# Wide lengths of q, and expert maxima row by row, in a fused attention and expert-routing kernel

## The chip, the cores and the metric

The program runs on one core of a Trainium2 chip. The metric is device time in microseconds (us) of one execution. TensorE is PE in the profile (PEld its weight loads), VectorE DVE, ScalarE ACT, GpSimd POOL and SyncE SP.

## What is computed

```
qn = q / (norm(q, axis=1) + 1e-6);  kn likewise          # q, k, v: 4 x 5056 x 256
s  = kn^T @ qn / tau                                     # 256 x 256 for each batch
a  = softmax(s, -1);  x = v @ a                          # 20224 tokens of 256
logits = x @ w_gate                                      # 8 experts
# pairs (token, expert) by falling logit: a token goes to the first expert that
# has room (2528 places each)
out[tokens of e] = relu(x @ w1[e]) @ w2[e]
```

## The kernel before

**Scores.** Four batches b run one after another. A batch has ten tiles of k and q (4 x 128 tokens each, buffers `ua` and `uc`). For each tile PE multiplies k by q into `s` (L334), ACT squares k and q (L344, L347) and DVE adds the squares into `acc_k` and `acc_q` (L348); L352 and L353 fold these to one row of 256. The lengths of batch b follow when the first tile of batch b+1 is in (`late(norms_before)`, L339).

**Lengths** (`norms`, L355, and `lengths`, L365). Four matmuls against a column of ones (L358) leave the 256 sums of k and the 256 of q as four columns, one sum a partition. On these 128x4 values run a copy out of PSUM (L361), a square root on ACT (L367), a step of Newton's rule on POOL and DVE (L368 to L373, the first reciprocal is L370), a second reciprocal (L375) and the factor 1/tau (L376).

**Softmax** (`softmax`, L379). The lengths of q are needed along the free axis. DVE makes two diagonals of them (L385), PE multiplies these by ones (L386) and ACT copies the result (L387). Then DVE scales the scores (L391), takes the row maximum, and works out the exponential as a polynomial (L396 to L405), the sums (L408) and the quotient `ac` (L414). PE turns `ac` (L422, `turned_a`), multiplies by the gate weights (L431, `gates`), ACT rounds it to `aH`, and DVE forms the rest `aL` (L249), which PE needs for x = v @ a (L283, with v split into `vh` and `vl`, L262). The transpose of batch 0 is put behind the last tile of batch 1, that of batch 3 stands behind all scores and the logits of one set of columns (L446).

**Order of the attention part.** The tile framework orders each engine's queue by its own estimates. All queues are served in order, and the softmax of batch b stands in DVE's queue among the additions of batch b+1.

**Routing** (`route`, L568). For R = 8, 7, ... 2 experts left: `m` is the maximum over R rows of logits L (L582); `eq` marks which row has it (L602), is multiplied by the codes 8, 7, ... of the rows (L604) and reduced to `f`, the code of a token's best expert (L607); `oh` is its one-hot form (L626 or L616). A search by 15 thresholds a round, with totals counted by 20 small matmuls (L699), finds which expert fills first and where. That expert's row is taken out by copying L to a second tile L2 (L876, L878). `compact` then lists its tokens.

**Order of the expert part.** From the last 26 tiles of x on, an `Order` object (L1035) plans by hand: each step of the routing names its engine and an estimated cost (`ve`, `vi`), and the plan puts it between the matmuls of the experts (`layer1` L1333, `layer2` L1365). x goes to DRAM (`store_x`) and is gathered by expert (L1225); the first expert can start when the last store has landed. 27 matmuls (L1313) stand in between.

Of the kernel before, what the change touches and what calls it, by code (L numbers as in the profile page):

```python
# [21 lines left out]
E, F = 8, 1024  # L22
# [69 lines left out]
def attention_moe(ctx: ExitStack, tc: tile.TileContext, q, k, vt, tau, wg, w1t, w2t, tabs, out):  # L92
# [74 lines left out]
    dmask = const.tile([128, CG, E], F32, name="dmask")  # L167
    V.tensor_scalar(dmask, jrow[:, 0:CG, None].to_broadcast([128, CG, E]), pc_, None, op0=OP.is_equal)
# [16 lines left out]
    scale = const.tile([128, 4], F32, name="scale")  # L185

    L2 = state.tile([128, E, COLS], F32, name="L1")
    U01 = state.tile([128, COLS], F32, name="U01")
    state.tile([128, 16], F32, name="pad_s")
# [108 lines left out]
    with ExitStack() as sctx:  # L298
# [12 lines left out]
        def scores(b, extra, norms_before):  # L311
# [183 lines left out]
        def load_scale():  # L495
            V.reciprocal(scale[:, 0:2], tau_t.to_broadcast([128, 2]))
            V.memset(scale[:, 2:4], 1.0)
# [70 lines left out]
    def route(p, R):  # L568
        nonlocal L, L2, U01, asg, ne, ne2
# [9 lines left out]
        else:  # L579
            m = rtile("m")  # L580
            yield ve(R * COLS)
            V.tensor_reduce(m, L[:, 0:R].rearrange("p r c -> p c r"), axis=AX.X, op=OP.max)  # L582
# [273 lines left out]
        if R > 1:  # L856
# [398 lines left out]
    def turn(p, c):  # L1255
# [4 lines left out]
        if not xts:  # L1260
            ffx.tile([128, 48], F32, name="pad_x", bufs=1)
# [299 lines left out]
```

## Time and profile before

| | us |
|---|---|
| median of 3 runs (lowest, highest) | 1256.83 (1256.02, 1259.64) |
| the profiled execution | 1257.59 |
| its span in the trace | 1255.8 |
| scores, softmax, x and logits up to the first routing step on DVE | 0 to 223 |
| the rest of x, the first expert's routing, the gather | 223 to 321 |
| experts | 321 to 1256 |

A row of the timeline gives start, length (of a pipelined instruction up to its end, so that rows overlap), engine, line, operation, output<-inputs, shapes, count, and in brackets the idle time before it and what ended that. A row of the groups gives busy time and mean nanoseconds of one.

### The profile page before, as it was taken

The numbers are of one execution on the slowest core, as the hardware profiler recorded it, in microseconds if no ns is written. First come the engines' busy times: TensorE is split into PE (matmuls) and PEld (weight loads), VectorE is DVE, ScalarE is ACT, GpSimd is POOL, SyncE is SP. The second block draws the span as 40 slices with busy tenths as digits, with TensorE's granted clock in tenths as the row PEclk, the third lists the DMA queues.
The fourth block names the chain that finished last, engine by engine and source line by source line (L and its number), as shares of the span: only waits on it lengthen the run. The fifth ranks groups of instructions, "written<-read, shape, count | busy, mean of one in ns | idle before, by whom it ended". The sixth has DMA issues, their size and how long they took to land.

```text
span 1255.8 us, 24082 instructions
## 1 busy us (share of the span) xinstructions
PE 1238.3 (99%) x8779; PEld 1111.2 (88%) x8779; DVE 872.7 (69%) x2457; ACT 601.0 (48%) x1441; POOL 384.5 (31%) x690
## 2 busy tenths in 40 slices
PE   8999999999999999999999999999999999999998
PEld 6888977898888988998999899988989898898998
DVE  6688496898778778868867888887785445344431
ACT  6646652467324434434533755556554554334331
POOL 1000010000432353244343452532444434334322
PEclk9999999999999999999999999999999999999999
DMA  8999875236112134143422532341434235333301
GB/s 308 314 409 414 311 275 199 118 153 235 58 48 87 41 84 121 42 90 81 126 68 59 138 79 64 80 131 40 93 73 129 59 80 146 73 69 76 69 31 34
DMA packets 184759, 160.33 MB, mean 128 GB/s; under 512 B 150080, under 2 KB 155328, under 8 KB 180032
## 3 DMA queue, kind: packets, MB, share of 16 engines
q1 hardware_dynamic: 157712, 79.33, 22.6%
q0 software_dynamic: 17664, 58.22, 14.4%
q10 hardware_dynamic: 9264, 21.24, 4.4%
q8 instruction: 69, 1.13, 0.4%
q14 instruction: 50, 0.41, 0.1%
HBM read 99.97 MB, written 41.68 MB: 113 GB/s over the span
## 4 chain that ended last, share of the span: by engine, by line
PE 84%; DVE 6%; issue 5%; POOL 2%; DMA 2%; ACT 1%; SPq 0%; POOLq 0%; DVEq 0%; ACTq 0%
PE ph L1333 33%; PE py L1365 32%; PE px L283 7%; PE s L334 7%; PE pc L699 2%; POOL out_dram L1372 1%; PE px L446 1%; DVE acc_q L348 1%; PE pi L912 1%; DVE yy L405 1%; DVE acc_k L348 1%; DMA x_d<-xs 1%; DMA ua<-in_q_dram 1%; DVE vl L262 0%; ACT ua L1184 0%
## 5 line engine op out<-in xcount | busy, mean ns | idle before, releaser
L1333 PE MATMUL ph<-xH,ua 128*128 128x512 f32 (+3 forms) x1312 | 354.8, 388 | 0.3 <-ACT xH L1300 0.3
L1365 PE MATMUL py<-uc,hH 128*128 128x256 f32 (+1 forms) x2560 | 334.5, 279 | 0.0
L1341 DVE SCALAR_TENSOR_TENSOR hL<-ph,hH 128x512 fp32r<-128x512 f32 (+3 forms) x328 | 219.4, 670 | 162.4 <-ACT hH L1336 158.2
L1365 PEld LDWEIGHTS py<-uc,hH 128*128 128x128 f32 (+1 forms) x2560 | 312.9, 187 | 2.2
L1372 POOL DMA_INDIRECT out_dram<-y,idx x160 | 162.0, 1013 | 498.1 <-ACT y L1370 445.3
L1336 ACT ACTIVATE hH<-ph 128x512 fp32r<-128x512 f32 (+3 forms) x328 | 190.6, 582 | 206.1 <-PE ph L1333 202.1
L1333 PEld LDWEIGHTS ph<-xH,ua 128*128 128x128 f32 x1312 | 238.4, 189 | 42.8 <-ACT xH L1300 0.4
L1333 PE MATMUL ph<-xL,ua 128*128 128x512 f32 (+3 forms) x656 | 201.3, 386 | 0.1
L1370 ACT ACTIVATE y<-py 128x256 f32<-128x256 f32 (+1 forms) x160 | 61.3, 383 | 251.0 <-PE py L1365 235.1
L1225 POOL DMA_INDIRECT xg<-x_d,src x156 | 156.6, 1004 | 71.6 <-issue 33.6
L1365 PE MATMUL py<-uc,hL 128*128 128x256 f32 (+1 forms) x1280 | 178.3, 280 | 0.0
L1365 PEld LDWEIGHTS py<-uc,hL 128*128 128x128 f32 (+1 forms) x1280 | 160.2, 187 | 0.0
L1333 PEld LDWEIGHTS ph<-xL,ua 128*128 128x128 f32 x656 | 122.1, 189 | 23.3 <-DVE xL L1303 0.3
L334 PE MATMUL s<-ua 128*128 128x256 f32 x320 | 73.7, 387 | 2.6 <-DMA ua<-in_q_dram 2.6
L334 PEld LDWEIGHTS s<-ua 128*128 128x128 f32 x320 | 61.0, 193 | 14.2 <-issue 3.4
L286 ACT ACTIVATE xs<-px 128x512 f32<-128x512 f32 (+1 forms) x96 | 49.4, 528 | 49.5 <-PE px L283 47.8
L334 PE MATMUL s<-uc 128*128 128x256 f32 x320 | 71.3, 380 | 0.0
L334 PEld LDWEIGHTS s<-uc 128*128 128x128 f32 x320 | 60.3, 190 | 8.8 <-issue 0.8
L283 PE MATMUL px<-aH,vh 128*128 128x256 f32 (+1 forms) x216 | 62.7, 292 | 0.0
L283 PE MATMUL px<-aH,vl 128*128 128x256 f32 (+1 forms) x216 | 61.3, 284 | 1.1 <-DVE vl L262 0.9
L1284 DVE TENSOR_TENSOR xL<-ph,xH 128x512 fp32r<-128x512 f32 (+1 forms) x66 | 42.9, 679 | 27.8 <-ACT xH L1281 25.7
L969 ACT ACTIVATE junk<-pi,rhalf 128x160 bf16<-128x160 f32 x140 | 54.0, 391 | 15.7 <-PE pi L912 14.6
(341 smaller groups left out, 1569.5 us busy)
## 6 DMA issues: line engine op xcount, KB each, us to landing
x_d<-xs ACTq DMA_DIRECT2D x39, 512.0 KB
xq<-xg SPq DMA_DIRECT2D x500, 32.0 KB
vr<-in_vt_dram SPq DMA_DIRECT2D x14, 1024.0 KB
uc<-in_k_dram SPq DMA_DIRECT2D x18, 512.0 KB
uc<-in_q_dram SPq DMA_DIRECT2D x18, 512.0 KB
ua<-in_k_dram SPq DMA_DIRECT2D x17, 512.0 KB
ua<-in_q_dram SPq DMA_DIRECT2D x17, 512.0 KB
out_dram<-y,idx POOLq DMA_INDIRECT x160, 2.4
```

The costliest lines, as they stand in the source:

```text
L283: mm = PE.matmul(px[:, i * C:i * C + width], lhsT=l_, rhs=a_, start=(j == 0), stop=(j == len(terms) - 1))
L286: S.activation(xs[:, t % TH:t % TH + n, 0:width], px[:, 0:n * width].rearrange("p (t c) -> p t c", t=n), AF.Copy)
L334: newest[0] = PE.matmul(sb[:, ib * C:(ib + 1) * C], lhsT=kt[:, t, ib * 128:(ib + 1) * 128], rhs=qt[:, t, :], start=(first and t == 0 and i ...
L969: S.activation(junk, pi[:, i * W:i * W + COLS], AF.Sign, bias=rhalf[:, g0 + i:g0 + i + 1], scale=-1.0, accum_out=sgn[:, g0 + i:g0 + i + 1])
L1225: P.indirect_dma_start(out=xg[:n, i, :], out_offset=None, in_=x_d, in_offset=bass.IndirectOffsetOnAxis(ap=at, axis=0))
L1284: V.tensor_tensor(xL[:, kb, 0:nt], pt[:, 0:nt], xH[:, kb, 0:nt].bitcast(F32), op=OP.subtract)
L1333: PE.matmul(ph[:, 0:nt], lhsT=l[:, w], rhs=x_[:, kb, 0:nt], start=(i == 0), stop=(i == 5))
L1336: S.activation(hH[:, fb, 0:nt], ph[:, 0:nt], AF.Relu)
L1341: V.scalar_tensor_tensor(hL[:, fb, 0:nt], ph[:, 0:nt], 0.0, hH[:, fb, 0:nt].bitcast(F32), op0=OP.max, op1=OP.subtract)
L1365: PE.matmul(py[:n, 0:C], lhsT=l[:, fb, tk], rhs=w[:, d], start=(j == 0), stop=(j == 23))
L1370: S.activation(y[:n], py[:n, 0:C], AF.Copy)
L1372: sd = P.indirect_dma_start(out=out, out_offset=bass.IndirectOffsetOnAxis(ap=idx[:n, col:col + 1], axis=0), in_=y[:n], in_offset=None)
```

## The change

Five edits. (1) `norms`: the sums of k stay two matmuls; the sums of q are made by one matmul with a 128x128 block of ones as weights, so that all partitions hold all 256 sums. (2) `lengths` runs on 128x258 values, with POOL keeping one of its five steps and DVE taking the rest; the diagonals, their matmuls and ACT's copy leave `softmax`. (3) `route`: the maxima over experts are trees of pairwise maxima (`tallest`), the codes and the one-hot rows are made by one instruction a row, `f` is bf16 and `oh` lies by rows in all rounds (which changes the operands of L699). (4) The finished row is taken out of L in place, without copy and without L2. (5) Small tiles for alignment change size.

```diff
             def norms():
                 pn = pcnt.tile([128, 512], F32, name="pc")
-                for i, (acc, ib) in enumerate(((acc_k, 0), (acc_k, 1), (acc_q, 0), (acc_q, 1))):
-                    newest[0] = PE.matmul(pn[:, i:i + 1], lhsT=acc[:, 0, ib * 128:(ib + 1) * 128], rhs=ones_f[:, 0:1],
-                                          start=True, stop=True)
-                nrm = wk.tile([128, 4], F32, name="nrm", bufs=2)
-                V.tensor_copy(nrm, pn[:, 0:4])
-                cur["rn"] = lengths(nrm)
+                for ib in range(2):
+                    PE.matmul(pn[:, ib:ib + 1], lhsT=acc_k[:, 0, ib * 128:(ib + 1) * 128], rhs=ones_f[:, 0:1],
+                              start=True, stop=True)
+                newest[0] = PE.matmul(pn[:, 2:2 + C], lhsT=ones_f, rhs=acc_q[:, 0], start=True, stop=True)
+                cur["rn"] = lengths(pn[:, 0:2 + C])
...
-        def lengths(nrm):
-            y = wk.tile([128, 4], F32, name="ny", bufs=2)
-            S.activation(y, nrm, AF.Sqrt)
+        def lengths(sums):
+            W = 2 + C
+            nrm = wk.tile([128, 2, C], F32, name="z").rearrange("p a c -> p (a c)")[:, 0:W]
+            V.tensor_copy(nrm, sums)
+            y = wk.tile([128, 2, C], F32, name="yy").rearrange("p a c -> p (a c)")[:, 0:W]
+            S.activation(y, sums, AF.Sqrt)
             P.tensor_scalar(y, y, 1.0e-30, None, op0=OP.max)
-            d = wk.tile([128, 4], F32, name="nd", bufs=2)
+            d = wk.tile([128, W], F32, name="rn")
             V.reciprocal(d, y)
-            P.tensor_tensor(d, d, nrm, op=OP.mult)
-            P.tensor_tensor(y, y, d, op=OP.add)
-            P.tensor_scalar(y, y, 0.5, 1.0e-6, op0=OP.mult, op1=OP.add)
-            rn = wk.tile([128, 4], F32, name="rn", bufs=2)
-            V.reciprocal(rn, y)
-            P.tensor_tensor(rn, rn, scale, op=OP.mult)
-            return rn
+            V.tensor_tensor(d, d, nrm, op=OP.mult)
+            V.tensor_tensor(y, y, d, op=OP.add)
+            V.tensor_scalar(y, y, 0.5, 1.0e-6, op0=OP.mult, op1=OP.add)
+            V.reciprocal(d, y)
+            V.tensor_tensor(d[:, 0:2], d[:, 0:2], scale, op=OP.mult)
+            return d
 
         def softmax(sb, rn):
             nf = wk.tile([128, 2, C], F32, name="nf")
-            dq = nf[:, 0].rearrange("p (j i) -> p j i", j=2)
-            rq = nf[:, 1]
-            pq = pcnt.tile([128, 512], F32, name="pc")
-            for jb in range(2):
-                V.tensor_scalar(dq[:, jb], ident, rn[:, 2 + jb:3 + jb], None, op0=OP.mult)
-                PE.matmul(pq[:, jb * 128:(jb + 1) * 128], lhsT=ones_f, rhs=dq[:, jb], start=True, stop=True)
-            S.activation(rq, pq[:, 0:C], AF.Copy)
+            rq = rn[:, 2:2 + C]
...
+    def tallest(out, rows, part, n, rate):
+        while n > 2:
+            h = (n + 1) // 2
+            yield ve(h * COLS, rate)
+            V.tensor_tensor(part[:, 0:h], rows[:, 0:h], rows[:, n - h:n], op=OP.max)
+            rows, n = part, h
+        yield ve(COLS)
+        V.tensor_tensor(out, rows[:, 0], rows[:, n - 1], op=OP.max)
...
-            V.tensor_reduce(m, L[:, 0:R].rearrange("p r c -> p c r"), axis=AX.X, op=OP.max)
+            top = rtile("eq", (128, E * COLS), BF).bitcast(F32).rearrange("p (r c) -> p r c", c=COLS)
+            yield from tallest(m, L, top, R, 1)
...
-            V.tensor_tensor(eq[:, 0:R], eq[:, 0:R], code9[:, 0:R, None].to_broadcast([128, R, COLS]), op=OP.mult)
-            f = rtile("f")
-            yield ve(R * COLS)
-            V.tensor_reduce(f, eq[:, 0:R].rearrange("p r c -> p c r"), axis=AX.X, op=OP.max)
+            for q in range(min(R, E - 1)):
+                yield (vi if q else ve)(COLS, 4)
+                V.tensor_scalar(eq[:, q], eq[:, q], float(E - q), None, op0=OP.mult)
+            f = rtile("f", dt=BF)
+            yield from tallest(f, eq, eq, R, 2)
...
+            oh = rtile("eq", (128, E * COLS), BF).rearrange("p (r c) -> p r c", r=E)
+            for q in range(Q):
+                yield (vi if q else ve)(COLS, 4)
+                V.tensor_scalar(oh[:, q], f, float(E - q), None, op0=OP.is_equal)
...
-                    PE.matmul(D, lhsT=ge[:, g], rhs=oh[:, cs_, 0:Q], start=(g == 0), stop=(g == COLS // CG - 1))
+                    PE.matmul(D, lhsT=ge[:, g], rhs=oh[:, 0:Q, cs_], start=(g == 0), stop=(g == COLS // CG - 1))
...
-            V.tensor_copy(L2[:, 0:R - 1], L[:, 1:R])
             yield ve((R - 1) * COLS)
-            V.copy_predicated(L2[:, 0:R - 1], keep[:, 0:R - 1, None].to_broadcast([128, R - 1, COLS]),
-                              L[:, 0:R - 1])
+            V.copy_predicated(L[:, 0:R - 1], drop[:, 0:R - 1, None].to_broadcast([128, R - 1, COLS]), L[:, 1:R])
```

DVE's queue behind the sums of batch 0, where its lengths are worked out among the additions of batch 1. Before:

```order
L361 COPY nrm<-pc 128x4
L348 TENSOR_TENSOR acc_k<-acc_k,sq 128x1024
L370 RECIPROCAL nd<-ny 128x4
L348 TENSOR_TENSOR acc_q<-acc_q,sq 128x1024
L375 RECIPROCAL rn<-ny 128x4
```

With the change (all lines from there on stand six lower):

```order
L366 COPY z<-pc 128x258
L347 TENSOR_TENSOR acc_k<-acc_k,sq 128x1024
L371 RECIPROCAL rn<-yy 128x258
L347 TENSOR_TENSOR acc_q<-acc_q,sq 128x1024
L372 TENSOR_TENSOR rn<-rn,z 128x258
L347 TENSOR_TENSOR acc_k<-acc_k,sq 128x1024
L373 TENSOR_TENSOR yy<-yy,rn 128x258
L347 TENSOR_TENSOR acc_q<-acc_q,sq 128x1024
L374 TENSOR_SCALAR yy<-yy 128x258
L347 TENSOR_TENSOR acc_k<-acc_k,sq 128x1024
L375 RECIPROCAL rn<-yy 128x258
```

The chain of the lengths has seven instructions on DVE in place of five, all but one 258 wide, with an addition behind nearly each of them.

The end of the same softmax on DVE, up to the folding of batch 1's sums (`acc_k`, `acc_q`). Before:

```order
L408 SCALAR_TENSOR_TENSOR yy,sm<-yy,pw 128x256 x2
L410 TENSOR_SCALAR sm<-sm 128x2
L348 TENSOR_TENSOR acc_k<-acc_k,sq 128x1024
L411 RECIPROCAL sm<-sm 128x2
L414 TENSOR_SCALAR ac<-yy,sm 128x256 x2
L348 TENSOR_TENSOR acc_q<-acc_q,sq 128x1024
L348 TENSOR_TENSOR acc_k<-acc_k,sq 128x1024
L348 TENSOR_TENSOR acc_q<-acc_q,sq 128x1024
L352 TENSOR_TENSOR acc_k<-acc_k 128x512
```

With the change:

```order
L402 SCALAR_TENSOR_TENSOR yy,sm<-yy,pw 128x256 x2
L347 TENSOR_TENSOR acc_q<-acc_q,sq 128x1024
L404 TENSOR_SCALAR sm<-sm 128x2
L351 TENSOR_TENSOR acc_k<-acc_k 128x512
L405 RECIPROCAL sm<-sm 128x2
L351 TENSOR_TENSOR acc_q<-acc_q 128x512
L408 TENSOR_SCALAR ac<-yy,sm 128x256 x2
L352 TENSOR_TENSOR acc_k<-acc_k 128x256
```

`ac` of batch 0 now stands behind every addition of batch 1; three of them stood behind it.

PE's queue where batch 0 ends and batch 1 begins, up to the transpose of `ac` (L422, now L416). Before:

```order
L358 MATMUL pc<-ones_f,acc_k 128x1 x2
L358 MATMUL pc<-ones_f,acc_q 128x1 x2
L334 MATMUL s<-uc 128x256 x8
L334 MATMUL s<-ua 128x256 x4
L386 MATMUL pc<-nf,ones_f 128x128 x2
L334 MATMUL s<-ua 128x256 x12
L334 MATMUL s<-uc 128x256 x16
L334 MATMUL s<-ua 128x256 x16
L334 MATMUL s<-uc 128x256 x16
L422 MATMUL pm<-ident,ac 128x128 x4
L334 MATMUL s<-ua 128x256 x8
```

With the change:

```order
L357 MATMUL pc<-ones_f,acc_k 128x1 x2
L359 MATMUL pc<-acc_q,ones_f 128x256
L333 MATMUL s<-uc 128x256 x8
L333 MATMUL s<-ua 128x256 x16
L333 MATMUL s<-uc 128x256 x16
L333 MATMUL s<-ua 128x256 x16
L333 MATMUL s<-uc 128x256 x16
L416 MATMUL pm<-ident,ac 128x128 x4
L333 MATMUL s<-ua 128x256 x8
```

The two matmuls of the diagonals are gone; the transpose keeps its place behind the last tile of batch 1.

## Rows read from the trace of the kernel before

**Rows 1.** The page, its first part: engines, busy time, share of the span.
```profile
PE 1238.3 (99%) x8779; PEld 1111.2 (88%) x8779; DVE 872.7 (69%) x2457; ACT 601.0 (48%) x1441; POOL 384.5 (31%) x690
```

**Rows 2.** PE's waits: who waited for whom, total, times, longest.
```profile
PE pc L386 <- DVE nf L385: 1.9, 2, 1.3
...
PE px L283 <- DVE vl L262: 0.9, 1, 0.9
```

**Rows 3.** Busy time of the engines by stretches of 20 us.
```profile
60.00:80.00 20.00, 20.00 (x95) 17.60 (x94) 19.93 (x36) 9.43 (x10) 0.61 (x1) 1.00 1.02 401
...
160.00:180.00 20.00, 20.00 (x117) 13.59 (x110) 19.97 (x31) 12.39 (x13) 1.68 (x2) 1.00 0.87 306
```

**Rows 4.** DVE's timeline, lengths of batch 0 to `aL` of batch 0.
```profile
47.66 0.16 DVE L361 COPY nrm<-pc 128x4 f32<-128x4 f32 x1 [7.49 <-PE pc L358]
...
79.39 0.62 DVE L414 TENSOR_SCALAR ac<-yy,sm 128x256 f32<-128x256 f32 x2
...
84.94 0.42 DVE L353 TENSOR_TENSOR acc_q<-acc_q 128x256 f32<-128x256 f32 x1
...
91.47 0.71 DVE L249 TENSOR_TENSOR aL<-ac,aH 128x528 fp32r<-128x528 f32 x1
```

**Rows 5.** PE's timeline of the same stretch.
```profile
54.18 0.68 PE L386 MATMUL pc<-nf,ones_f 128*128 128x128 f32 x4 [1.27 <-DVE nf L385]
...
80.60 0.60 PE L422 MATMUL pm<-ident,ac 128*128 128x128 f32 x4
...
85.17 0.58 PE L358 MATMUL pc<-ones_f,acc_k 128*128 128x1 f32 x4 [0.42 <-DVE acc_k L353]
...
92.29 0.33 PE L283 MATMUL px<-aL,vh 128*128 128x264 f32 x1
```

**Rows 6.** All instructions of lines L370 and L411: ns shortest/median/longest.
```profile
L370 DVE RECIPROCAL nd<-ny x4: 178/178/179, 50.2 to 195.5; 128x4 f32<-128x4 f32 x4
...
L411 DVE RECIPROCAL sm<-sm x4: 150/157/166, 79.2 to 211.8; 128x2 f32<-128x2 f32 x4
```

**Rows 7.** Groups of DVE's instructions by line and form: busy us, mean ns.
```profile
L348 DVE TENSOR_TENSOR acc_k<-acc_k,sq 128x1024 f32<-128x1024 f32 x36 | 43.8, 1216 | 19.3 <-ACT sq L347 18.3 <-ACT acc_k L344 1.0
...
L582 DVE TENSOR_REDUCE m<-L 128x160 f32<-128x1280 f32 x1 | 2.4, 2397 | 0.1
...
L385 DVE TENSOR_SCALAR nf<-ident,rn 128x128 f32<-128x128 f32 x8 | 2.0, 282 | 0.7 <-POOL rn L376 0.6
...
L410 DVE TENSOR_SCALAR sm<-sm 128x2 f32<-128x2 f32 x4 | 0.6, 162 | 0.1
```

**Rows 8.** Timeline of DVE and PE, lengths of batch 2 to `ac` of batch 3.
```profile
156.01 0.16 DVE L361 COPY nrm<-pc 128x4 f32<-128x4 f32 x1 [8.58 <-PE pc L358]
...
192.09 0.42 DVE L353 TENSOR_TENSOR acc_q<-acc_q 128x256 f32<-128x256 f32 x1
...
193.70 0.50 PE L358 MATMUL pc<-ones_f,acc_k 128*128 128x1 f32 x4
...
199.66 0.87 DVE L391 SCALAR_TENSOR_TENSOR z<-s,rn,nf 128x256 f32<-128x256 f32 x2 [2.12 <-ACT nf L387]
...
212.48 0.81 PE L422 MATMUL pm<-ident,ac 128*128 128x128 f32 x4 [0.28 <-DVE ac L414]
```

**Rows 9.** Single us around the first expert: PE busy first, granted clock third from last.
```profile
320.00:321.00 1.00, 0.55 (x4) 0.41 (x4) 1.00 (x1) 0.54 (x2) 0.00 (x0) 1.00 0.00 0
...
323.00:324.00 1.00, 1.00 (x7) 1.00 (x6) 0.51 (x2) 0.46 (x2) 0.65 (x1) 0.50 0.00 0
326.00:327.00 1.00, 1.00 (x9) 1.00 (x8) 0.77 (x2) 0.42 (x2) 0.57 (x2) 0.83 0.00 0
```

**Rows 10.** Timeline: ACT's last copy of x, POOL's first gather.
```profile
311.56 0.60 ACT L286 ACTIVATE xs<-px 128x512 f32<-128x512 f32 x1 [0.61 <-PE px L283]
...
316.08 0.95 POOL L1225 DMA_INDIRECT xg<-x_d,src  x1 [23.50 <-DVE eq L602]
```

**Rows 11.** The page's chain of work that ended last: its time by line.
```profile
PE ph L1333 33%; PE py L1365 32%; PE px L283 7%; PE s L334 7%; PE pc L699 2%; POOL out_dram L1372 1%; PE px L446 1%; DVE acc_q L348 1%; PE pi L912 1%; DVE yy L405 1%; DVE acc_k L348 1%; DMA x_d<-xs 1%; DMA ua<-in_q_dram 1%; DVE vl L262 0%; ACT ua L1184 0%
```

More of the change, by code (lines that the diff above doesn't have):

```diff
@@ L166, in attention_moe @@
     V.memset(jsel[:, NT:J], 0.0)
-    dmask = const.tile([128, CG, E], F32, name="dmask")
-    V.tensor_scalar(dmask, jrow[:, 0:CG, None].to_broadcast([128, CG, E]), pc_, None, op0=OP.is_equal)
+    dmask = const.tile([128, CG], F32, name="dmask")
+    V.tensor_scalar(dmask, jrow[:, 0:CG], pc_, None, op0=OP.is_equal)
     th0 = const.tile([128, NT, CG], I16, name="th0")
@@ L184, in attention_moe @@
     tau_t = const.tile([128, 1], F32, name="tau_t")
-    scale = const.tile([128, 4], F32, name="scale")
-    L2 = state.tile([128, E, COLS], F32, name="L1")
+    scale = const.tile([128, 2], F32, name="scale")
     U01 = state.tile([128, COLS], F32, name="U01")
-    state.tile([128, 16], F32, name="pad_s")
+    state.tile([128, 72], F32, name="pad_s")
     asg = state.tile([128, COLS], F32, name="asg")
@@ L495, in load_scale @@
         def load_scale():
-            V.reciprocal(scale[:, 0:2], tau_t.to_broadcast([128, 2]))
-            V.memset(scale[:, 2:4], 1.0)
+            V.reciprocal(scale, tau_t.to_broadcast([128, 2]))
         cur = {}
@@ L568, in route @@
     def route(p, R):
-        nonlocal L, L2, U01, asg, ne, ne2
+        nonlocal L, U01, asg, ne, ne2
         r = {}
@@ L602, in route @@
             V.tensor_tensor(eq[:, 0:R], L[:, 0:R], m[:, None, :].to_broadcast([128, R, COLS]), op=OP.is_equal)
-            yield ve(R * COLS)
-            V.tensor_tensor(eq[:, 0:R], eq[:, 0:R], code9[:, 0:R, None].to_broadcast([128, R, COLS]), op=OP.mult)
-            f = rtile("f")
-            yield ve(R * COLS)
-            V.tensor_reduce(f, eq[:, 0:R].rearrange("p r c -> p c r"), axis=AX.X, op=OP.max)
+            for q in range(min(R, E - 1)):
[3 more added lines that the diff above has]
+            yield from tallest(f, eq, eq, R, 2)
             yield ve(COLS)
@@ L611, in route @@
             Q = R if few else R + R % 2
-            flat = rtile("eq", (128, E * COLS), BF)
-            yield ve(Q * COLS)
+            oh = rtile("eq", (128, E * COLS), BF).rearrange("p (r c) -> p r c", r=E)
+            for q in range(Q):
+                yield (vi if q else ve)(COLS, 4)
+                V.tensor_scalar(oh[:, q], f, float(E - q), None, op0=OP.is_equal)
             if few:
-                oh = flat.rearrange("p (r c) -> p r c", r=E)
-                V.tensor_tensor(oh[:, 0:R], f[:, None, :].to_broadcast([128, R, COLS]),
-                                code9[:, 0:R, None].to_broadcast([128, R, COLS]), op=OP.is_equal)
                 need = rtile("need", (128, E))
@@ L624, in route @@
             else:
-                oh = flat.rearrange("p (c r) -> p c r", r=E)
-                V.tensor_tensor(oh[:, :, 0:Q], f[:, :, None].to_broadcast([128, COLS, Q]),
-                                code9[:, None, 0:Q].to_broadcast([128, COLS, Q]), op=OP.is_equal)
                 Ex = rtile("Ex", (128, J, E), F32R)
@@ L694, in totals @@
                 pc = pcnt.tile([128, 512], F32, name="pc")
-                D = pc[:, 0:CG * Q]
+                D = pc[:, 0:Q * CG].rearrange("p (r c) -> p r c", c=CG)
                 yield "P", COLS * Q / 2.4 + 3 * COLS / CG + 60
@@ L698, in totals @@
                     cs_ = slice(g * CG, (g + 1) * CG)
-                    PE.matmul(D, lhsT=ge[:, g], rhs=oh[:, cs_, 0:Q], start=(g == 0), stop=(g == COLS // CG - 1))
+                    PE.matmul(D, lhsT=ge[:, g], rhs=oh[:, 0:Q, cs_], start=(g == 0), stop=(g == COLS // CG - 1))
                 yield ve(CG * Q, psum=True)
-                Dm = rtile("Dm", (128, CG, E))
-                V.tensor_tensor(Dm[:, :, 0:Q], D.rearrange("p (c r) -> p c r", r=Q), dmask[:, :, 0:Q], op=OP.mult)
+                Dm = rtile("Dm", (128, E, CG))
+                V.tensor_tensor(Dm[:, 0:Q], D, dmask[:, None, :].to_broadcast([128, Q, CG]), op=OP.mult)
                 yield ve(CG * Q)
                 Dr = rtile("Dr", (128, E))
-                V.tensor_reduce(Dr[:, 0:Q], Dm[:, :, 0:Q].rearrange("p c r -> p r c"), axis=AX.X, op=OP.add)
+                V.tensor_reduce(Dr[:, 0:Q], Dm[:, 0:Q], axis=AX.X, op=OP.add)
                 yield ve(J * Q)
@@ L797, in route @@
             V.tensor_scalar(one, code9, cs, None, op0=OP.is_equal)
-            keep = rtile("keep", (128, 8), I32)
+            drop = rtile("drop", (128, 8), I32)
             yield ve(8)
-            V.tensor_scalar(keep, code9[:, 0:8], cs, None, op0=OP.is_gt)
+            V.tensor_scalar(drop, code9[:, 0:8], cs, None, op0=OP.is_le)
             Gf = rtile("Gf")
@@ L871, in route @@
             yield ve(16)
-            V.tensor_copy(ne2[:, :, 0:8], o9[:, :, 1:9])
+            V.tensor_copy(ne2[:, :, 0:8], o9[:, :, 0:8])
             yield ve(16)
-            V.copy_predicated(ne2[:, :, 0:8], keep[:, None, :].to_broadcast([128, 2, 8]), o9[:, :, 0:8])
-            yield ve((R - 1) * COLS, 2)
-            V.tensor_copy(L2[:, 0:R - 1], L[:, 1:R])
+            V.copy_predicated(ne2[:, :, 0:8], drop[:, None, :].to_broadcast([128, 2, 8]), o9[:, :, 1:9])
             yield ve((R - 1) * COLS)
-            V.copy_predicated(L2[:, 0:R - 1], keep[:, 0:R - 1, None].to_broadcast([128, R - 1, COLS]),
-                              L[:, 0:R - 1])
-            L, L2, ne, ne2 = L2, L, ne2, ne
+            V.copy_predicated(L[:, 0:R - 1], drop[:, 0:R - 1, None].to_broadcast([128, R - 1, COLS]), L[:, 1:R])
+            ne, ne2 = ne2, ne
     def compact(p):
@@ L1259, in turn @@
         nt = n_of(p, c)
-        if not xts:
-            ffx.tile([128, 48], F32, name="pad_x", bufs=1)
         xH = ffx.tile([128, 2, 512], F32R, name="xH")
```

## The prediction

> **What bounds the kernel now.** I read the page's busy times first: PE is busy 99% of the span, DVE 69% [rows 1]. So the time can fall only by what PE idles or runs at half clock, or by fewer columns on PE. The list of PE's waits says how little there is to win where the change works: 1.9 us in all at the diagonals (L386), 0.9 us for `vl` [rows 2]. The busy times by stretches say the opposite about risk: between 60 and 80 us DVE is busy 19.93 us of 20, between 160 and 180 us 19.97 [rows 3]. There DVE is as full as PE, and has kept up only just. The average of 69% hides it, since it comes from the experts' part. What the change adds on DVE in these stretches is not covered; it moves what PE waits for.
>
> Which waits end last there? The timelines of DVE and PE, batch 0's lengths to its `aL`, show it [rows 4, 5]. DVE makes `ac` at 79.39 us, and PE comes to its transpose at 80.60: about 0.6 us to spare. `aL` starts at 91.47 and takes 0.71; PE's first matmul with it starts at 92.29. Again nothing to spare. For batches 2 and 3 [rows 8]: DVE folds the last sums of batch 3 at 192.09 (+0.42), PE works out the norms at 193.70, the scaling follows at 199.66, the transpose at 212.48. So lateness in `ac` or `aL` goes straight to PE.
>
> **The change, part by part.** *(1) The wide lengths, price.* What PE does is near a draw: two one-column matmuls of `acc_q` and the two of the diagonals (0.68 us with a wait of 1.27 ahead [rows 5]) against one 256 wide. On DVE the two reciprocals grow from 4 to 258 elements a partition, which no row shows. The rows nearest: 128x4 takes 178 ns each time, 128x2 takes 150, 157 or 166 [rows 6]. Two elements more cost 12 ns (against 166) to 21 (against the median) or 28 (against 150): 6, 10.5 or 14 ns an element, thus for 254 more 1.70, 2.85 or 3.73 us a reciprocal. Other work on DVE grows far less: 162 ns at 128x2 (L410), 282 at 128x128 (L385) [rows 7], 0.42 us at 128x256 (L353) [rows 4]: about 1 ns an element, by which a wide reciprocal would cost 0.44 us. That is the lower bound, 3.73 the upper. I take 8.25 ns, the middle between the two like rows (6 and 10.5), since RECIPROCAL's own rows are nearer than another operation's: 178 + 254 x 8.25 = 2.27 us.
>
> Three rows with 2 and 4 elements are thin support for a slope, and they alone can't exclude that the difference is overhead. The Trainium skill, page "VectorE: DVE Perf Modes", section "First, the fixed hardware budget", speaks against the change here: the reciprocal is an iterative divide with a repeat count of 8 in the same pipe; at the page's 0.96 GHz 8 cycles are, as an estimate from that page, 8.3 ns an element, 2.29 us for 258 and the same sum as mine, where the slope of the other DVE rows gives about 1260. No run so far shows a wide one.
>
> *DVE's work a batch.* After: copy 0.42, reciprocals 2 x 2.27, two TENSOR_TENSORs 2 x 0.42, one TENSOR_SCALAR 0.28, scale 0.16: 6.24 us (the size of each by L353, L385 and L410). Before: copy 0.16, reciprocals 2 x 0.18, diagonals 2 x 0.28: 1.08 us. So 5.16 us more, four times. The square root on ACT and POOL's one step become wide as well; they stand beside DVE's additions (1.22 us each [rows 7]) while DVE is full, so I cost them at nothing there.
>
> *(a) Batch 0's `ac`.* DVE's order now has `ac` behind the last folding of batch 1, which ended at 84.94 + 0.42 = 85.36 [rows 4]. Two foldings (0.84) and one split of v (as `aL`, about 0.7) moved behind it. New end of `ac`: 85.36 + 5.16 - 1.54 = 89.0. PE would reach its transpose at 80.60 - 1.27 - 0.68 = 78.65, so it idles some 10 us, and the transpose is 8.4 late. Even if reciprocals cost 0.44 it would be at about 85.3, after PE.
>
> *(b) Its `aL`.* From the transpose PE needs 85.17 - 80.60 - 0.42 = 4.15 us to the norms of batch 1 [rows 5]: now 93.15. Those take 0.9, and then copy, an addition, a reciprocal, and an addition stand ahead of `aL` on DVE: 93.15 + 0.9 + 0.42 + 1.22 + 2.27 + 1.22 + 0.71 = 99.9, with hops between engines 100.5, where it was ready for 92.29: 8.2 late. The wait for `vl` of 0.9 [rows 2] and other small slack go into that; I take +7 as what stays for batch 2.
>
> *(c) Batches 2 and 3.* From the copy of batch 2's norms (156.01) to the end of batch 3's sums (192.51) DVE had 36.5 us with hardly a gap [rows 8, 3]. That starts 7 later and holds some 5 more: 204.2 instead of 192.51. PE comes some 2 us earlier than that and waits.
>
> *(d) The end.* Norms to scaling took 199.66 - 193.70 = 5.96 us, 2.12 of it DVE's wait for the diagonals' way over PE and ACT [rows 8]. Now 5.96 + 5.16 - 2.12 = 9.0, less 0.5 for three steps that POOL gives up (chosen, between -1.5 and, if its wide step and the root are dear, +1): 8.5. Scaling to transpose stays 12.82. 204.2 + 8.5 + 12.82 = 225.5 against 212.48: PE is some 13 late; I take 12.8, as PE can begin the norms a little before DVE's queue is empty. PE has other work (logits, x) for part of that and idles the rest, some 5 us. Behind it PE has work without waits and gives nothing back.
>
> *(e) The clock.* Where PE had idled (busy 0.55 us of the one from 320), the row at 323 has PE fully busy and granted 0.50, i.e. 1.2 instead of 2.4 GHz, and at 326 still 0.83 [rows 9]. Some 3.4 us at half level cost 1.7. After the idle times of (a), (b) and (d) I count that 2 to 3 times: +4.0 (bounds 0 and 5.1).
>
> *(2) Routing.* The first round's chain gets shorter: `m` was one reduction of 2.40 us [rows 7], three pairwise steps should take 1.6; codes, `f` and one-hot rows save about 2 by the same count. But the gather starts at 316.08, after the last x tile (copied at 311.56, behind PE [rows 10]) has been stored, not after DVE; and rounds 2 to 8 lie beside the experts on a PE that is 99% busy. DVE's later savings (some 16 us by such counts) are covered by PE, and L2's copies likewise. A shorter chain can fill some of the last gaps ahead of the gather: -1.5 (bounds 0 and -2.5).
>
> *(3) L699's operand* has the same columns in another order: 900 matmuls, 176 to 206 ns, 2% of the chain [rows 11]. I take 0; the upper bound is that a strided read halves its rate: +25 us, as 2% of the span is 25.
>
> *(4), (5)* In place instead of copied, and tile sizes: cover as in (2), 0.
>
> Sum: +12.8 + 4.0 - 1.5 = +15.3 on the profiled execution's 1257.59, which is 0.8 above the median: 1272.9, as a median **1272**. One us of a wide reciprocal is worth some 7 us: two in (a), one in (b), two in (c), two in (d). 1.70 gives 1268, 2.85 gives 1276, 3.73 with a full clock loss 1283.
>
> **The rivals.**
> - *Reciprocal nearly flat* (0.44 us). For: all other DVE rows. Against: two elements already show 12 to 28 ns. Then (a) still idles 6 us, since `ac` stands behind the last folding; the rest nearly closes: +4 -1.5, 1260. Chance 0.10.
> - *Dearer*: 14 ns an element, or three clock losses and wide POOL and ACT steps on the path at the end: 1279 to 1286. For: the 150 row. Chance 0.08.
> - *The other side: DVE still delivers in time.* If a wide reciprocal costs under some 0.4 us and DVE gets to `ac` before PE (78.65), the waits for the diagonals (1.9), their matmuls (four batches, some 0.5 each net) and part of the gap before the gather go: 1253. It decides at DVE's load: 6 us less than I count in 30 of a full queue. Against: the full stretches [rows 3]. Chance 0.05.
> - *The strided operand halves L699*: +25 on top, 1297. For: nothing in the trace, it has only one form. Chance 0.05.
>
> **How the numbers follow.** My case has 0.72, its own range 1266 to 1279 (slope 6 to 10.5, clock 2 to 3 times, the end's -1.5 to +1). The flat and dear cases are taken in: 1259 to 1282. Left out are the other side, the strided operand, and the dear case's far end, under 0.15. About 0.3% (3.8 us) is what a measurement of this kernel can tell from no change: faster 0.05, same 0.07 (most of the flat case), slower 0.88.
>
> **What would show it.** RECIPROCAL 128x258 near 2.3 us; DVE without gaps from the lengths of batch 0 to `ac`, PE idle some 10 us before its first transpose, some us before `aL`, and some 5 before the last transpose; granted clock 0.5 behind these; L699 at 176 to 206 ns as before; the gap between the last x and the gather little changed. I am wrong if the reciprocal is under 1 us, if `ac` of batch 0 comes at 79, if PE stays busy from 60 to 225, or if the experts take less PE time than before.

## The result, and the profile after

| | before | changed |
|---|---|---|
| median us, runs taken together (lowest, highest) | 1257.48 (1256.02, 1259.64) | 1269.53 (1269.10, 1271.58) |
| ratio, 95% interval | | 1.0097 (1.0084 to 1.0110) |
| profiled execution, its span | 1257.59, 1255.8 | 1271.58, 1269.6 |

The change makes the kernel 12 us slower; 1272 was forecast. The profiled execution is 2 us above the median of its kernel. The page's first line for the changed kernel, against [rows 1]:

```profile
PE 1243.5 (98%) x8755; PEld 1115.7 (88%) x8755; DVE 872.8 (69%) x2534; ACT 600.9 (47%) x1437; POOL 379.0 (30%) x674
```

DVE's total is the same as before to a tenth of a us. What the wide lengths add, the shorter routing takes off, but in different stretches: only the stretches tell. All instructions of the two wide reciprocals (shortest, median, longest ns), against [rows 6]:

```profile
L371 DVE RECIPROCAL rn<-yy x4: 1766/1766/1768, 51.1 to 206.6; 128x258 f32<-128x258 f32 x4
...
L375 DVE RECIPROCAL rn<-yy x4: 1757/1762/1767, 58.1 to 209.7; 128x258 f32<-128x258 f32 x4
```

From 178 ns at 4 elements to 1766 at 258: 6.25 ns an element, near the lowest of the three slopes taken from [rows 6]. Busy time by stretches, against [rows 3] (PE first, DVE third):

```profile
60.00:80.00 20.00, 18.90 (x87) 16.07 (x86) 20.00 (x30) 10.01 (x11) 0.52 (x1) 1.00 1.02 389
180.00:200.00 20.00, 20.00 (x100) 16.13 (x100) 20.00 (x34) 9.99 (x10) 0.52 (x1) 1.00 0.74 253
```

DVE has no idle time left in either. PE's timeline of the changed kernel, against [rows 5] and the end of [rows 8]:

```profile
47.57 3.62 PE L333 MATMUL s<-uc 128*128 128x256 f32 x16
...
74.45 7.14 PE L333 MATMUL s<-uc 128*128 128x256 f32 x32 [0.76 <-DMA uc<-in_q_dram]
86.83 1.16 PE L416 MATMUL pm<-ident,ac 128*128 128x128 f32 x4 [5.24 <-DVE ac L408]
87.79 4.77 PE L333 MATMUL s<-ua 128*128 128x256 f32 x16
92.39 0.50 PE L357 MATMUL pc<-ones_f,acc_k 128*128 128x1 f32 x4
...
99.84 0.39 PE L282 MATMUL px<-aL,vh 128*128 128x264 f32 x1 [0.46 <-DVE aL L248]
...
203.13 0.58 PE L357 MATMUL pc<-ones_f,acc_k 128*128 128x1 f32 x4 [0.58 <-DVE acc_k L352]
...
223.57 1.16 PE L416 MATMUL pm<-ident,ac 128*128 128x128 f32 x4 [4.04 <-DVE ac L408]
...
235.60 7.17 PE L282 MATMUL px<-a,ub 128*128 128x256 f32 x32
```

The last of these in the kernel before:

```profile
221.97 7.17 PE L283 MATMUL px<-a,ub 128*128 128x256 f32 x32
```

Read it by how late each place is. Transposes of batch 0: 86.83 for 80.60, +6.2. Norms of batch 1: +7.2. First use of `aL`: +7.6. Norms of batch 3: +9.4. Transposes of batch 3: +11.1. Then the x tiles: they begin at 235.60, before at 221.97, +13.6, and the program ends 13.8 later. All of it arises before 236 us; what follows has its old length.

Two kinds of loss stand in these rows. One is the brackets: 5.24 and 4.04 us for `ac`. The other is the pace behind them: the 8 score matmuls at 87.79 (two records each) took 4.77 us, and the 8 at 47.57 only 3.62. Single us (granted clock third from last):

```profile
86.00:87.00 1.00, 0.17 (x1) 0.17 (x1) 1.00 (x4) 0.00 (x0) 0.00 (x0) 0.85 1.00 422
87.00:88.00 1.00, 1.00 (x5) 0.92 (x6) 1.00 (x4) 0.00 (x0) 0.00 (x0) 0.50 1.03 430
88.00:89.00 1.00, 1.00 (x3) 0.79 (x3) 0.31 (x1) 0.97 (x2) 0.00 (x0) 0.50 0.98 401
...
229.00:230.00 1.00, 1.00 (x12) 0.32 (x8) 0.00 (x0) 0.00 (x0) 0.00 (x0) 0.50 0.00 0
230.00:231.00 1.00, 1.00 (x13) 0.24 (x8) 0.40 (x1) 0.00 (x0) 0.00 (x0) 0.97 0.00 0
```

From 87 on PE is fully busy at 1.2 GHz. The clock falls at 86.7, while PE still waits, and is back at 90.1. It is at half again from 100.4 to 103.8 and from 223.2 to 230.0.

And DVE at the end of batch 0's softmax, against [rows 4]:

```profile
83.96 1.22 DVE L347 TENSOR_TENSOR acc_q<-acc_q,sq 128x1024 f32<-128x1024 f32 x1
85.10 0.16 DVE L404 TENSOR_SCALAR sm<-sm 128x2 f32<-128x2 f32 x1
85.17 0.68 DVE L351 TENSOR_TENSOR acc_k<-acc_k 128x512 f32<-128x512 f32 x1
85.77 0.15 DVE L405 RECIPROCAL sm<-sm 128x2 f32<-128x2 f32 x1
85.85 0.67 DVE L351 TENSOR_TENSOR acc_q<-acc_q 128x512 f32<-128x512 f32 x1
86.43 0.61 DVE L408 TENSOR_SCALAR ac<-yy,sm 128x256 f32<-128x256 f32 x2
```

No row has a bracket: DVE waits for nothing, its queue is simply long. `ac` begins at 86.43, before at 79.39.

### The profile page after: what moved, and what is told of

Read it like the earlier page. It is cut to its first block, busy times and chain, and to the rows that moved or that the text cites. A ratio compares the mean times of both kernels' runs of the same rounds, so it can differ in the third digit from the quotient of the medians.

```text
span 1269.6 us, 24082 instructions
## 1 busy us (share of the span) xinstructions
PE 1243.5 (98%) x8755; PEld 1115.7 (88%) x8755; DVE 872.8 (69%) x2534; ACT 600.9 (47%) x1437; POOL 379.0 (30%) x674
## 4 chain that ended last, share of the span: by engine, by line
PE 80%; DVE 8%; issue 5%; DMA 3%; POOL 2%; ACT 2%; POOLq 0%; SPq 0%; ACTq 0%; DVEq 0%
PE py L1358 31%; PE ph L1326 31%; PE px L282 7%; PE s L333 5%; PE pc L697 2%; DVE acc_q L347 2%; DMA x_d<-xs 2%; DVE acc_k L347 1%; POOL out_dram L1365 1%; PE pi L907 1%; DMA ua<-in_q_dram 1%; DVE yy L399 1%; PE px L440 1%; DMA xg<-x_d,src 1%; DVE rn L375 0%
## 5 line engine op out<-in xcount | busy, mean ns | idle before, releaser
L282 PE MATMUL px<-aL,vh 128*128 128x256 f32 (+1 forms) x216 | 62.1, 287 | 0.5 <-DVE aL L248 0.5
```

The source lines that it names most:

```text
L282: mm = PE.matmul(px[:, i * C:i * C + width], lhsT=l_, rhs=a_, start=(j == 0), stop=(j == len(terms) - 1))
```

## The experiments

Every run was compared with runs of the kernel before on the same chip (medians 1257.05 for the first four, 1257.36 for the next four, 1257.41 and 1257.76 for the rest).

**Which half of the change.** First the changed kernel again, then each half alone.

> The changed kernel unaltered, for a second profile. Median 1269.5 us within 0.8. Profile: RECIPROCAL 128x258 at 1.76 to 1.77 us; PE idle 5.2 us before the transposes of batch 0 and 4.0 before those of batch 3. If the 2 us by which the first profiled execution was above the median came from the 7.3 us at half clock after the transposes of batch 3 (223.6 to 230.9 us), that stretch is 3 to 4 us here and the execution at 1269.5; if it is again 7 us, the 2 us came from elsewhere.

Measured 1270.20 (1270.08 to 1271.39). The stretch at half clock behind batch 3's transposes is not shorter; it begins at 221.9 and lasts to 232.1:

```profile
231.00:232.00 1.00, 1.00 (x8) 0.20 (x4) 0.58 (x2) 0.00 (x0) 0.00 (x0) 0.50 0.00 0
232.00:233.00 1.00, 1.00 (x16) 0.37 (x12) 0.00 (x0) 0.00 (x0) 0.00 (x0) 0.94 0.00 0
```

So the 2 us of the first profile came from elsewhere. Read in finer windows, the first profile's stretch there lasted 6.8 us (223.2 to 230.0) and not the 7.3 of the expectation, and this one's 10.2. The stretches lie elsewhere too: here 6.8 us behind batch 0's transposes (85.4 to 92.2), none at 100 and none at the first expert, where the first profile has 3.4 (336 to 339 us), as [rows 9] do. In all both profiles have 17.1 us at half clock, but PE was busy in 15.9 of them in the first and in 13.2 in this one; half of the 2.7 us between is 1.3, which is what the two profiled executions differ by (1271.58 and 1270.29). A stretch of 3.4 us in which PE is busy thus costs some 1.7, and it comes and goes between executions.

The kernel before with `norms`, `lengths` and `softmax` as changed, and `route` as before:

> The kernel before with the wide lengths alone (routing as before). Theory (two wide reciprocals a batch in a full DVE queue make ac late, the rest of the change is hidden): 1269 to 1271 us, the whole of the +12. Rival (routing in the new form costs or gains some of it): 1263 to 1266 if it costs 4 to 6 us, 1273 or more if it hides a gain of 3.

Measured 1270.90, ratio 1.0112 (1.0095 to 1.0129): the whole loss.

The changed kernel with `norms`, `lengths` and `softmax` as before, and `route` as changed:

> The changed kernel with the lengths of before (routing in the new form). Theory: 1256.5 to 1258 us, no difference from the kernel before that can be measured. Rival, the new routing gains once PE does not wait for other things: 1251 to 1255. Rival, the operand by rows or the greater number of instructions costs: 1261 or more.

Measured 1258.93, ratio 1.0015 (1.0006 to 1.0025): neither gain, nor the 4 us of the rival, but 1.9 us over the kernel before, 0.9 more than theory's upper end. In its profile PE's wait for the first expert's list grew (its waits, against 0.5 us on the same line before):

```profile
PE pi L913 <- ACT ext L934: 1.3, 1, 1.3
```

and half clock stands behind batch 3's transposes (214.9 to 218.3), where the kernel before had full clock. That is not all of it: its two runs with a mean granted clock of 1.000 took 1257.58 and 1258.22, the three such runs of the kernel before beside them 1255.82 to 1256.30. With the wide lengths the sign turns (1270.20 with the new routing, 1270.90 with the old; and the last pair below). So the routing is worth about 2 us either way, and doesn't explain 12.

**Is it the divide?**

```diff
-            V.reciprocal(d, y)
+            V.tensor_scalar(d, y, 1.0 / 5056.0, None, op0=OP.mult)
```

(both of them)

> The changed kernel with both wide reciprocals replaced by a TENSOR_SCALAR of the same width (a multiplication by 1/5056, so that the lengths are only near their values). Theory: 1.48 us less twice a batch, at some 7 us for each us: 1259 us (1257 to 1262), ac of batch 0 by 83 us, and under 2 us of PE's idle time before its transposes. Rival (width, hops to ACT and POOL and the order of ac behind the folding cost, not the divide): 1266 or more.

Measured 1254.55 (1252.79 to 1259.59), ratio 0.9988 (0.9977 to 1.0000): lower than expected, and 15.6 us under the changed kernel. So with the divides gone all else that the change does to the lengths, POOL's wide step and the width of the other steps with it, costs nothing, and may gain 2. `ac` is ready just after PE:

```profile
80.91 0.62 DVE L408 TENSOR_SCALAR ac<-yy,sm 128x256 f32<-128x256 f32 x2
...
83.71 0.69 DVE L351 TENSOR_TENSOR acc_k<-acc_k 128x512 f32<-128x512 f32 x1
...
81.32 0.81 PE L416 MATMUL pm<-ident,ac 128*128 128x128 f32 x4 [0.35 <-DVE ac L408]
```

DVE's order moved too: `ac` stands ahead of the foldings again, so this kernel alone doesn't separate order and duration; the next one bears on it.

**Is it the queue, or the chain?** The kernel before, with reciprocals that nobody waits for:

```diff
-            V.reciprocal(rn, y)
+            made = V.reciprocal(rn, y)
...
+            for _ in range(2):
+                with tc.issue_after(made.ins):
+                    V.reciprocal(spare, spare)
```

> The kernel before with two more reciprocals of 128x258 a batch on a scratch tile that nobody reads, put in DVE's queue right behind the lengths. If the load on DVE's queue is what costs (theory): 3.5 us more a batch, 1264 to 1268 us, with ac of batch 0 after 81 us and PE waiting for it, and the scaling of batch 3 later. If only the length of the chain through the lengths costs (rival): 1256.5 to 1259.

Measured 1270.12, ratio 1.0105 (1.0088 to 1.0122). Two divides a batch (1.74 us each) on a scratch tile cost as much as the whole change. DVE's rows, and PE's with the same waits as in the changed kernel:

```profile
52.04 1.73 DVE L382 RECIPROCAL spare<-spare 128x258 f32<-128x258 f32 x1
53.69 0.18 DVE L391 TENSOR_SCALAR nf<-ident,rn 128x128 f32<-128x128 f32 x1
53.81 1.77 DVE L382 RECIPROCAL spare<-spare 128x258 f32<-128x258 f32 x1
...
57.86 0.87 DVE L397 SCALAR_TENSOR_TENSOR z<-s,rn,nf 128x256 f32<-128x256 f32 x2
...
83.31 0.61 DVE L420 TENSOR_SCALAR ac<-yy,sm 128x256 f32<-128x256 f32 x2
...
84.97 0.68 DVE L352 TENSOR_TENSOR acc_k<-acc_k 128x512 f32<-128x512 f32 x1
...
83.71 0.81 PE L428 MATMUL pm<-ident,ac 128*128 128x128 f32 x4 [3.54 <-DVE ac L420]
...
98.68 0.59 PE L283 MATMUL px<-aL,vh 128*128 128x264 f32 x1 [2.18 <-DVE aL L249]
```

The scaling in the kernel before:

```profile
56.42 0.87 DVE L391 SCALAR_TENSOR_TENSOR z<-s,rn,nf 128x256 f32<-128x256 f32 x2
```

Nobody reads the spare divides, but each stands ahead of a diagonal in DVE's queue, so they hold up the lengths as well, and queue and chain are not parted as cleanly as meant. For batch 0 the queue is the larger part: the scaling begins 1.4 us later than before (57.86 for 56.42), `ac` 3.9 later (83.31 for 79.39 [rows 4]). `ac` stands ahead of the foldings here, as before, so its place behind them is not needed for the loss. That the time came out above what was expected fits the end, where from batch 3's norms to its scaling 9.2 us pass (202.16 to 211.36) instead of 5.96; this was not tested by itself.

**How steep is it?** One divide in place of two (Newton's rule, the 1e-6 beside the norm left out), and a leaner form of it:

```diff
             V.reciprocal(d, y)
+            V.tensor_tensor(nrm, nrm, d, op=OP.mult)
+            V.tensor_tensor(nrm, nrm, d, op=OP.mult)
+            V.tensor_scalar(nrm, nrm, -0.5, 1.5, op0=OP.mult, op1=OP.add)
             V.tensor_tensor(d, d, nrm, op=OP.mult)
-            V.tensor_tensor(y, y, d, op=OP.add)
-            V.tensor_scalar(y, y, 0.5, 1.0e-6, op0=OP.mult, op1=OP.add)
-            V.reciprocal(d, y)
```

> The changed kernel with the second wide reciprocal replaced by three multiplications and one multiply-add (Newton's rule for the reciprocal root; the 1e-6 beside the norm is left out). DVE's work for the lengths falls from 5.24 to 3.9 us a batch, 1.34 less. By the slope between the changed kernel and the one without divides (15.6 us for 2.96) that is 7 us: 1263 (1261 to 1265). If it is a threshold, with all of the loss at one order of the queue: 1256 or 1269.

Measured 1265.50, ratio 1.0066 (1.0049 to 1.0082): half a us above the range, and far from both values of the threshold.

```diff
-            V.tensor_copy(nrm, sums)
...
-            S.activation(y, sums, AF.Sqrt)
-            P.tensor_scalar(y, y, 1.0e-30, None, op0=OP.max)
+            S.activation(y, sums, AF.Sqrt, bias=floor)
...
             V.reciprocal(d, y)
-            V.tensor_tensor(d, d, nrm, op=OP.mult)
-            V.tensor_tensor(y, y, d, op=OP.add)
-            V.tensor_scalar(y, y, 0.5, 1.0e-6, op0=OP.mult, op1=OP.add)
-            V.reciprocal(d, y)
+            V.scalar_tensor_tensor(y, sums, -0.5, d, op0=OP.mult, op1=OP.mult)
+            V.tensor_tensor(y, y, d, op=OP.mult)
+            V.scalar_tensor_tensor(d, y, 1.5, d, op0=OP.add, op1=OP.mult)
```

> As the last, and leaner: the sums read from PSUM without the copy, the floor given as the square root's bias in place of POOL's wide step, three fused DVE steps behind the one reciprocal (the 1e-6 beside the norm is left out). DVE's work for the lengths is 3.2 us a batch, and POOL's 0.85 to 1.48 us leave the chain. By the same slope 1259; with POOL's step gone from the end of batch 3's lengths 1 us less: 1258 (1255 to 1260). Rival (one wide divide a batch is enough to keep DVE late): 1263.

Measured 1259.19, ratio 1.0014 (1.0004 to 1.0023), within the range. In a row, with DVE's work for the lengths of one batch as counted from the rows:

| kernel | us of DVE a batch | median us |
|---|---|---|
| before | 1.08 | 1257.4 |
| no divide | 2.3 | 1254.6 |
| lean, one divide | 3.2 | 1259.2 |
| one divide | 3.9 | 1265.5 |
| before, two spare divides | 4.6 | 1270.1 |
| changed | 5.2 | 1270.2 |

The kernel with 2.3 us a batch loses nothing. From there on each us a batch, four in all, costs 5.4 on average (15.6 for 2.9), unevenly from row to row. It is a rough slope: the kernels differ in more than DVE's work (the lean one has no step on POOL, the one with spare divides has the old routing).

**Where PE stands.** Batch 0's transposes moved on PE behind the norms of batch 1:

```diff
+                if b == 2:
+                    def norms(first=norms):
+                        first()
+                        cur["aT"] = turned_a(cur["ac"])
                 if b < B - 1:
-                    put(GATES_AT[b - 1], turn_a)
+                    if b > 1:
+                        put(GATES_AT[b - 1], turn_a)
```

> The changed kernel with batch 0's transposes put on PE behind the 8 score matmuls and the norms of batch 1 that stood behind them. Theory (PE stands at the transposes while work that needs nothing is queued behind): the wait of 4.9 to 5.2 us falls under 1.5 and the half clock after it goes: 1264 to 1266. Rival (DVE's queue alone sets the pace, the wait turns up again at aL or at the end): 1269 or more.

Measured 1265.87, ratio 1.0070 (1.0053 to 1.0086), as the theory had it. PE does the score matmuls in the time, and waits less (1.27 us, for the sums); the 4 us at batch 3 stay:

```profile
87.71 0.58 PE L357 MATMUL pc<-ones_f,acc_k 128*128 128x1 f32 x4 [1.27 <-DVE acc_k L352]
...
219.29 1.17 PE L416 MATMUL pm<-ident,ac 128*128 128x128 f32 x4 [4.05 <-DVE ac L408]
```

**The clock by itself.** PE kept busy while it waits:

```diff
+        def fill_pe(acc, n):
+            hot = pcnt.tile([128, 512], F32, name="pc")
+            for _ in range(n):
+                newest[0] = PE.matmul(hot[:, 0:128], lhsT=ones_f, rhs=acc, start=True, stop=True)
...
+                    if b == 1:
+                        late(fill_pe, jrow, 18)
...
+        late(fill_pe, jrow, 15)
```

(ahead of batch 0's transposes and of batch 3's)

> The changed kernel with matmuls that nobody reads (18 of 128x128 ahead of batch 0's transposes, 15 ahead of batch 3's), some 3.9 and 3.3 us of PE's idle 4.9 and 4.1. PE waits for the same ac at the same time, but does not idle. If the clock after the idle time costs by itself (theory): no granted 0.50 behind both transposes, 1.7 us at the first and 3.6 to 4.5 at the second come back: 1264.5 (1263 to 1266). Rival (the time behind the transposes is bound by other engines, the low clock only goes with it): 1269 or more.

Measured 1265.63, ratio 1.0073 (1.0056 to 1.0090). PE's timeline:

```profile
80.09 4.18 PE L414 MATMUL pc<-jrow,ones_f 128*128 128x128 f32 x36
86.72 0.81 PE L421 MATMUL pm<-ident,ac 128*128 128x128 f32 x4 [2.46 <-DVE ac L408]
87.37 3.62 PE L333 MATMUL s<-ua 128*128 128x256 f32 x16
90.83 0.50 PE L357 MATMUL pc<-ones_f,acc_k 128*128 128x1 f32 x4
...
219.54 0.81 PE L421 MATMUL pm<-ident,ac 128*128 128x128 f32 x4 [0.65 <-DVE ac L408]
```

Batch 0's transposes begin when they did (86.72 for 86.83), and PE is 1.6 us earlier at the norms, with the 8 score matmuls in 3.62 us. No stretch of half clock is left around either place. Work for nothing gave back 4.6 us (from 1270.20; 3.9 from 1269.53): about a third of the loss was the clock. Not quite all of this is the clock alone, since around batch 3's transposes the framework also ordered PE's matmuls otherwise (14 of the 16 of one group of logits now stand behind the transposes).

**A version that beats both?** The lean lengths with the later transposes, the same with the routing of before, and the first of them with fillers (4 matmuls ahead of the first x, 31 in place of 27 ahead of the first expert).

> The lean lengths (one reciprocal, 1e-6 left out) together with the later transposes of batch 0, routing in the new form. Theory: the wait of 2.67 us before the transposes goes, and with it the 3.4 us at half clock behind it (1.7 us): 1255 us (1253.5 to 1257), below both kernels. Rival (the wait turns up again at the norms or at the first x): 1258 to 1260.

Measured 1256.81 (1255.42 to 1266.39), ratio 1.0009 (0.9994 to 1.0024): the transposes' wait is gone as the theory has it, and with it 2.4 us of the lean kernel's 1259.19, but the median is at the upper end of its range and not below the kernel before by anything that can be measured. PE still waits 4.0 us for loads of the scores (its waits; the lean kernel 4.2, the kernel before 2.6), and its clock falls to half behind 0.95 us of idle time ahead of the first x:

```profile
PE s L335 <- DMA ua<-in_q_dram: 2.4, 2, 1.8
PE s L335 <- DMA uc<-in_q_dram: 1.6, 2, 0.8
```

> The same with the routing of before. If the new routing costs what the kernel with the new routing alone showed (1.9 us in its medians): 1253 us (1252 to 1255), under the last one by 1 to 2.5. If that was a half-clock stretch at batch 3's transposes that comes and goes with small shifts, and the routing is worth nothing: the same within 0.7.

Measured 1258.86, ratio 1.0014 (1.0005 to 1.0022): 2 us above the last one, outside both expectations. Beside the old lengths the old routing was 1.9 us better, here it is 2 worse. The profiles of the two have the same two stretches of half clock and lie 0.4 us apart (1258.78 and 1259.16). In the runs with a mean granted clock of 0.999 or 1.000 the last one took 1255.4 to 1257.1 and this one 1256.9 to 1258.1, so about 1 us of the 2 is left at like clock; it stays open.

> The lean lengths with the later transposes, and the two places filled where that kernel's profile shows granted 0.50: four matmuls of 128x128 ahead of the first x, and 31 in place of 27 of the matmuls ahead of the first expert. Theory: 1.7 us come back at the first place, and 1.7 at the second in those executions that showed it: 1254 (1252.5 to 1256), clearly below the kernel before. Rival: the idle time left is still enough to lose the clock, or the fillers only push the work back: 1257 to 1258.

Measured 1257.16 (1256.36 to 1257.58), ratio 0.9995 (0.9986 to 1.0004), where the rival had it. Its profile has full clock at both places and a span of 1254.5, so the clock was kept in that execution. All eleven runs show a mean granted clock of 0.999 or 1.000 and lie between 1256.36 and 1257.58, where without the fillers they went from 1255.42 to 1266.39 at 0.967 to 1.000. So the fillers took away the late executions and made none of the early ones earlier; why not stays open. No version that works out the lengths clearly beat the kernel before.

## Why the prediction was right

**The main reason held.** DVE's queue was full in [rows 3], and the divide of 258 elements lengthened it. Shown from three sides: without the divide the loss is gone, spare divides that nobody reads make it, and it grows with DVE's work.

**The price of the divide** was taken as 2.27 us and is 1.77, near the lower like slope (1.70), far from the flat bound of 0.44. So DVE's work a batch grew by 4.2 us and not 5.16. The Trainium skill, page "VectorE: DVE Perf Modes", section "First, the fixed hardware budget", has the reciprocal as an iterative divide with a repeat count of 8. The trace bears out that it is dear (1.77 us, where a copy of the same width takes 0.43); but the 8.3 ns an element, an estimate from that page with a cycle for each repeat, are a third above the measured 6.25, and the measurement stands.

**Step (a)** was late by 6.2 us, 8.4 were forecast, and one part of it failed. I let PE reach the transposes at 78.65, since the wait for the diagonals and their matmuls were gone. It was there at 86.83 - 5.24 = 81.6. Loads took the place of the removed wait, 0.97, 0.34 and (above, at 74.45) 0.76 us for `uc` and `ua`, where the transfers already ran at a share of 1.02 [rows 3]:

```profile
59.06 7.14 PE L333 MATMUL s<-uc 128*128 128x256 f32 x32 [0.97 <-DMA uc<-in_q_dram]
66.54 7.14 PE L333 MATMUL s<-ua 128*128 128x256 f32 x32 [0.34 <-DMA ua<-in_q_dram]
```

That was in the rows, and I didn't ask what the earlier PE would run into. The idle time was therefore 5 us and not 10; the end of `ac`, 87.04, was 2 before the forecast 89.0, by the cheaper divides.

**Steps (b) to (d).** 7 us were to stay for batch 2; its norms came at 162.55 instead of 155.02, +7.5. PE idled 0.46 us for `aL`, not some us. Batch 3's sums: 203.3, forecast 204.2; PE waited 0.58 us for them and not 2, since 1.89 us of matmuls for x stand ahead of the norms now. Norms to scaling: 8.53 us (203.13 to 211.66), forecast 8.5. Transposes: 11.1 late, forecast 12.8.

**Step (e), the clock,** was put at 4.0; fillers gave 3.9 to 4.6 back, so the size was about right. Its place in the sum was not. Batch 0's transposes to batch 1's norms took 1.4 us longer (5.56 for 4.15), the stretch at 100 us cost about 1.6 of PE time, and batch 3's transposes to the x tiles took 2.5 longer (12.03 for 9.49; 3.7 in the second profile, 13.24). The first two lie ahead of batch 3's transposes, so they are inside the 11.1 that these are late, and only the third comes on top: 11.1 + 2.5 = 13.6.

**The sum.** With the fillers 7.9 us of the loss are left (1265.63 for 1257.76), and that is what the lateness of (a) to (d) is worth without the clock; it was put at 12.8. By the prediction's own 7 us for each us of a reciprocal the cheaper divide makes 3.5 of the 5 us between; the rest was not traced. So 7.9 + 4.6 and no gain by the routing stand against 12.8 + 4.0 - 1.5. The sum came within 2.5 us in part by luck: a lateness 5 us too large was made up for by a gain of the routing that did not come and a clock 0.6 dearer. The same 7 us for each us, taken without the clock, made the expectation for the kernel without divides too high: 1.48 us are 10.4 by it, with 4.6 of the clock 15.0 (an estimate), and 15.6 were measured.

**Routing** was put at -1.5. The three pairs with old and new routing give +1.9, -0.7 and -2.0, so no gain that holds. Its chain did get shorter: 7.7 us for `m`, codes, `f` and one-hot rows became 4.6 in the first round. But the gather begins as before some 4 us behind the last copy of x, against [rows 10]:

```profile
325.34 0.60 ACT L285 ACTIVATE xs<-px 128x512 f32<-128x512 f32 x1 [0.61 <-PE px L282]
...
329.48 0.98 POOL L1220 DMA_INDIRECT xg<-x_d,src  x1 [24.48 <-DVE eq L607]
```

That is 4.1 us, before 4.5. The bracket names one row of DVE's, but the gather waits for the stores of x as well, and its distance to the last copy has hardly moved; the 3 us that the chain lost were not what it waited for. The matmuls with the one-hot rows, before and with the change ([rows 11] has their share):

```profile
L699 PE MATMUL pc<-eq,ge x900: 176/183/206, 235.9 to 673.7; 128*128 128x64 bf16 x72, 128*128 128x48 bf16 x72, 128*128 128x32 bf16 x36
...
L697 PE MATMUL pc<-eq,ge x900: 176/183/263, 248.2 to 680.5; 128*128 128x64 bf16 x72, 128*128 128x48 bf16 x72, 128*128 128x32 bf16 x36
```

The median is the same, so the order of the operand's rows has no price that shows.

**The rivals with a cheap divide** were two: 1260 at 0.44 us, with `ac` still behind the last folding, and 1253 at under some 0.4 us, with `ac` there before PE. The kernel without divides (0.29 us in their place) took 1254.55, near the second, though its `ac` came 0.35 us after PE. The prediction held the order of DVE's queue fixed; with less work in it `ac` stands ahead of the foldings, so the first rival's 1260 and its `ac` at 85.3 were too late.

## What to carry to other kernels

Read an off-path engine's load by stretches, not over the span: 69% hid a queue without a gap, and 3.5 us a batch of work that nobody read, 14 in all, cost 13 us. Before an operation is made wider, ask for its price per element; among DVE's operations here the divide grows at 6 ns an element and the others at about 1. When a wait is removed, ask what the engine runs into next (here the loads), and when one is added, count the clock behind it as well, once.

## What was not expected of the hardware

Behind batch 3's transposes TensorE stayed at 1.2 GHz for 6.8 us, and for 10.2 in two other profiles (the changed kernel's second, and the lengths alone). Behind most other idle times it was 3.4 us, but 6.8 behind batch 0's transposes in the changed kernel's second profile. Part of the longer stretches PE was fully busy (from 225.3 to 232.1 in that profile). What makes them longer was not tried. Whether the first expert runs at half clock differs between executions of one and the same kernel, and moves its time by some 1.7 us; differences under 2 us between these variants are of that size.
